# Storing whole output rows for two of four batches, and starting the right half's products between the left half's outputs

## The chip, the cores and the metric

The program runs on one core of one Trainium2 chip, from one launch. A core has a matrix engine (TensorE, PE in the profile, with weight loads shown apart as PEld), a vector engine (DVE), a scalar engine (ACT), GpSimd (POOL), and SyncE (SP), which here issues every transfer. The transfers run on 16 DMA engines between HBM and the on-chip buffer SBUF; matrix products land in a small accumulation memory, PSUM, and have to be copied to SBUF by ACT or DVE before they can be stored. The metric is device microseconds (us) of one execution.

## The reference

Three layers in a row, all in float32, with 4 batches of 448 tokens (1792 rows) and a width of 768:

```python
scores = scale * (q @ k.T) - log(S); x = sigmoid(scores) @ v       # 4 x 12 heads, 448 x 64
x = ((x @ w_a) * (x @ w_b)) @ w_out                                # 1792 x 768, inner 1536
logits = x @ phi                                                   # 1792 x 32 slots
d = softmax of logits over the tokens;  slot_input = d.T @ x       # 32 x 768
for e in range(8):                                                 # 4 slots for each expert
    slot_out[e] = relu(slot_input[e] @ w1[e]) @ w2[e]              # 768 -> 1024 -> 768
c = softmax of logits over the slots
return c @ slot_out                                                # 1792 x 768
```

Only the last two lines are of interest here: the product with w2 gives 32 slot rows of 768 columns, and each of the 1792 tokens gets a weighted sum of those rows. The output is 1792 x 768 x 4 bytes = 5.5 MB.

## The kernel before, in words

One long function, `body`, writes all engines' instructions in program order; a helper (`tc.manual_schedule`) keeps that order on each engine and adds the semaphore waits. Attention, the two large products and the routing statistics take the first 620 us. What follows is bound to the expert weights w1 and w2, which are streamed through a ring of SBUF tiles: `order0`, `order1` and `order2` (L662 to L664) list the transfers, `pump` issues the next one when a ring slot is free, and `done` frees the slots whose tiles have been multiplied.

The end of the program, L813 to L865, is what the change touches:

- `COLS` cuts the 768 output columns into a left half (h = 0) and a right half (h = 1) of 384. The last `NCOL` = 8 entries of `order2`, each 768 KB, are loaded as halves too: L693 issues the eight left halves (384 KB each), then L696 issues the eight right halves. In this document R1 to R8 are those right halves, in order.
- `w2_product(n, halves)` (L816) multiplies four ring tiles, two weight rows of each, into the accumulators `sps[h]` of the halves asked for: eight products for each half, which PE runs as 16 instructions. The last eight tiles take two calls for each half.
- For each half (loop of L844): two calls of `w2_product` finish the sum, then a chain follows with one instruction at a time: a copy out of PSUM (L848, by ACT for the left half and DVE for the right one), a product with `selF` that adds up the four partial sums (L850), a copy again (L851). Then for each chunk `c` of 112 tokens and each batch `b` one small product (L859, two PE instructions) and one copy (L861, ACT for even batches, DVE for odd ones) into an output tile of SBUF. Six PSUM buffers are used in turn (`tags`), so a product waits for the copy of the sixth product before it.
- The left half is stored after every second chunk, for each batch 112 x 2 x 384 numbers (336 KB, L865): 8 transfers, L1 to L8. The right half is stored after each chunk, 112 x 384 numbers (168 KB, L863): 16 transfers. In HBM a stored piece is a run of 384 numbers, 1536 bytes, and the DMA moves it as one packet.

SP issues its transfers in program order, and each waits for the transfer eight places ahead of it to have landed, since eight semaphores are used in turn. On each of the 16 DMA engines transfers are worked off in the order of their issue.

Of the kernel before, what the change touches and what calls it, by code (L numbers as in the profile page):

```python
# [9 lines left out]
F32 = mybir.dt.float32  # L10
# [8 lines left out]
B, H, S, D = 4, 12, 448, 64  # L19
DM, FF, NS, NE, F = 768, 1536, 32, 8, 1024  # L20
C = 4
T = S // C
# [11 lines left out]
def body(ctx, tc, q, k, v, w_a, w_b, w_out, phi, w1, w2, out):  # L34
    nc = tc.nc
    pe, act, dve, pool, sp = nc.tensor, nc.scalar, nc.vector, nc.gpsimd, nc.sync
# [17 lines left out]
    def ps_tile(tag, shape, bufs):  # L54
        return psp.tile(shape, F32, tag=tag, name=tag, bufs=bufs)
# [6 lines left out]
    def ms(shape=(128, S)):  # L62
        tags = banks[run["banks"]]
        tag = tags[run["ms"] % len(tags)]
        run["ms"] += 1
        return ps_tile(tag, list(shape), 4 if tag == "sc" else 2)
# [597 lines left out]
    order2 = [("w2", g, x, j) for g in range(2) for x in range(KE // 2) for j in range(4)]  # L664
    queue = order0 + order1 + order2
    NCOL = 8
    ring, slots, rest = {}, [], []
# [102 lines left out]
    for what in order0:  # L770
        i = what[1]
        h, n, f0 = (0, 4, 4 * i) if i < 3 else (1, 6, 6 * (i - 3))
# [43 lines left out]
    def w2_product(n, halves):  # L816
        _, g, x, _ = order2[n]
        for i in range(2):
            for h in halves:
                c0, w = COLS[h]  # L820
                for j in range(4):
                    pe.matmul(sps[h][32 * j:32 * j + 32], hT[:, 2 * x + i, 2 * j + g],  # L822
                              ring[order2[n + j]][0][:, i, c0:c0 + w],
                              start=(g == 0 and x == 0 and i == 0),
                              stop=(g == 1 and x == KE // 2 - 1 and i == 1))
# [7 lines left out]
    s4, s4r = small[:, :DM], small[:, DM:2 * DM]  # L833
    evac = (act.copy, dve.tensor_copy)
    ov = out.rearrange("(b c p) n -> b p c n", b=B, c=C)
    ob = [[], []]
    for h in range(2):
        for b in range(B):
            pl, nm = slots.pop(0)
            ob[h].append(pl.tile([128, 2048], F32, tag=nm, name="o")[:T, :C * (DM // 2)].rearrange(  # L840
                "p (c n) -> p c n", c=C))
    tags = ("sc", "sc", "sc", "sc", "ms", "ms")
    k = 0
    for h, (c0, w) in enumerate(COLS):  # L844
        for n in range(len(order2) - NCOL, len(order2), 4):
            w2_product(n, (h,))

        evac[h](s4[:, c0:c0 + w], sps[h])  # L848
        t = ms((128, w))
        pe.matmul(t, selF.rearrange("p j s -> p (j s)"), s4[:, c0:c0 + w], start=True, stop=True)  # L850
        evac[h](s4r[:, c0:c0 + w], t)  # L851
        for c in range(C):
            op = []
            for b in range(B):
                tag = tags[k % 6]
                op.append(ps_tile(tag, [T, w], 4 if tag == "sc" else 2))
                k += 1
                r = slice(32 * b, 32 * b + 32)
                pe.matmul(op[b], cT[r, c * T:(c + 1) * T], s4r[r, c0:c0 + w], start=True, stop=True)  # L859
            for b in range(B):  # L860
                evac[b % 2](ob[h][b][:, c], op[b])  # L861
                if h:
                    sp.dma_start(out=ov[b][:, c, c0:c0 + w], in_=ob[h][b][:, c])  # L863
                elif c % 2:
                    sp.dma_start(out=ov[b][:, c - 1:c + 1, c0:c0 + w], in_=ob[h][b][:, c - 1:c + 1])  # L865


# [23 lines left out]
```

## Time and profile before

| | us |
|---|---|
| median of 3 runs (730.11 to 732.01) | 731.52 |
| the profiled execution, its own time | 727.57 |
| span of the profiled execution | 725.5 |
| PE busy | 682.7 (94%) |
| DVE busy, ACT busy | 310.2, 272.0 |
| expert weights and output: DMA engines without a break | from about 633 to the end |

The profiled execution is some 4 us faster than the median of the runs; its own time is 2.07 us over its span. The times in the rows count from the start of the span. The table of engines would call this a PE kernel, but it is an average: PE is the busiest engine for the first 630 us and the DMA engines are for the last 90. The profile's strip of 40 slices (18 us each) shows the change-over, and tables of stretches of 2 us show what holds in the part that the change touches. A DMA share over 1 comes from packets that overlap on one engine.

### The profile page before, as it was taken

The numbers are of one execution on the slowest core, as the hardware profiler recorded it, in microseconds if no ns is written. First come the engines' busy times: TensorE is split into PE (matmuls) and PEld (weight loads), VectorE is DVE, ScalarE is ACT, GpSimd is POOL, SyncE is SP. The second block draws the span as 40 slices with busy tenths as digits, with TensorE's granted clock in tenths as the row PEclk, the third lists the DMA queues.
The fourth block names the chain that finished last, engine by engine and source line by source line (L and its number), as shares of the span: only waits on it lengthen the run. The fifth ranks groups of instructions, "written<-read, shape, count | busy, mean of one in ns | idle before, by whom it ended". The sixth has DMA issues, their size and how long they took to land.

```text
span 725.5 us, 10845 instructions
## 1 busy us (share of the span) xinstructions
PE 682.7 (94%) x4231; PEld 487.8 (67%) x4231; DVE 310.2 (43%) x452; ACT 272.0 (37%) x469; POOL 246.6 (34%) x151
## 2 busy tenths in 40 slices
PE   6999998999999999999999999999999999997684
PEld 4446667777777677688776876877888896433132
DVE  3557998899863323333333232312323232300022
ACT  4778678778643504214135042231201011100021
POOL 0116766666672332233323332323444442100000
PEclk9999999999999999999999999999999999999998
DMA  9967999889962432422414322220689945999998
GB/s 217 196 162 229 301 291 282 280 277 296 298 200 57 128 97 74 128 78 73 133 50 133 106 58 79 88 66 0 243 275 323 366 152 204 394 415 418 412 362 275
DMA packets 107474, 148.99 MB, mean 205 GB/s; under 512 B 51360, under 2 KB 84384, under 8 KB 104352
## 3 DMA queue, kind: packets, MB, share of 16 engines
q1 hardware_dynamic: 107424, 148.31, 63.0%
q8 instruction: 33, 0.54, 0.3%
q14 instruction: 17, 0.14, 0.1%
HBM read 128.46 MB, written 19.83 MB: 204 GB/s over the span
## 4 chain that ended last, share of the span: by engine, by line
PE 77%; DMA 13%; ACT 4%; DVE 3%; issue 1%; POOL 1%; SPq 0%; ACTq 0%; POOLq 0%
PE ab L492 46%; PE sc L193 9%; DMA e<-in_moe_w 9%; PE sc L179 7%; PE ms L147 3%; PE ms L469 2%; ACT a L183 1%; PE ms L455 1%; PE ab L179 1%; PE ms L569 1%; DMA kn<-in_k 1%; DMA out<-w 1%; DVE gk L317 1%; DMA wr_all<-in_moe_w_b 1%; ACT gk L304 1%
## 5 line engine op out<-in xcount | busy, mean ns | idle before, releaser
L420 POOL TENSOR_TENSOR wl<-wr_all,wh 128x768 fp32r<-128x768 f32 x50 | 92.4, 1849 | 204.8 <-DVE wh L419 122.6
L492 PE MATMUL ab<-xh,wh 128*128 128x448 f32 x576 | 142.0, 376 | 1.4 <-ACT wh L419 1.4
L492 PE MATMUL ab<-xh,wl 128*128 128x448 f32 x576 | 141.7, 376 | 0.0
L492 PE MATMUL ab<-xl,wh 128*128 128x448 f32 x576 | 136.2, 371 | 0.0
L492 PEld LDWEIGHTS ab<-xh,wh 128*128 128x128 f32 x576 | 103.2, 188 | 20.9 <-issue 10.9
L492 PEld LDWEIGHTS ab<-xh,wl 128*128 128x128 f32 x576 | 104.0, 188 | 18.3 <-issue 8.6
L492 PEld LDWEIGHTS ab<-xl,wh 128*128 128x128 f32 x576 | 105.9, 188 | 15.5 <-issue 7.3
L183 ACT ACTIVATE a<-sc,nlog 112x448 f32<-112x448 f32 x168 | 93.6, 639 | 59.6 <-PE sc L179 55.9
L322 POOL TENSOR_TENSOR w<-gk,cy 128x768 int32<-128x768 int32 x36 | 66.3, 1841 | 99.5 <-DVE gk L317 72.7
L504 DVE TENSOR_TENSOR misc<-misc,ab 128x448 f32<-128x448 f32 x48 | 29.7, 618 | 127.5 <-PE ab L492 127.4
L501 ACT COPY misc<-ab 128x448 f32<-128x448 f32 x48 | 25.8, 538 | 153.2 <-PE ab L492 148.4
L193 PE MATMUL sc<-a,vn 112*64 112x448 f32 x384 | 76.1, 544 | 0.0
L420 POOL TENSOR_TENSOR wl<-wr,wh 128x768 fp32r<-128x768 f32 x22 | 40.5, 1840 | 53.7 <-DVE wh L419 45.7
L193 PEld LDWEIGHTS sc<-a,vn 112*64 112x64 f32 x384 | 26.0, 137 | 41.5 <-issue 38.7
L419 DVE CAST wh<-wr_all 128x768 fp32r<-128x768 f32 x50 | 35.1, 701 | 37.3 <-POOL wl L420 22.9
L420 POOL TENSOR_TENSOR wl<-w,wh 128x768 fp32r<-128x768 f32 x24 | 45.0, 1873 | 3.0 <-ACT wh L419 3.0
L822 PE MATMUL ab<-e,gk 128*32 128x384 f32 x240 | 34.2, 531 | 11.9 <-DMA e<-in_moe_w 11.7
L204 ACT ACTIVATE xh<-sc 128x448 fp32r<-128x448 f32 x24 | 13.1, 544 | 71.6 <-PE sc L193 71.6
L315 DVE TENSOR_SCALAR mf<-gk 128x768 f32<-128x768 f32 x36 | 34.1, 947 | 9.0 <-ACT gk L304 8.7
L205 DVE TENSOR_TENSOR xl<-sc,xh 128x448 fp32r<-128x448 f32 x24 | 15.0, 623 | 52.3 <-ACT xh L204 52.3
L179 PE MATMUL sc<-qh,kh 64*112 64x448 f32 x168 | 34.9, 411 | 0.6 <-ACT qh L140 0.6
L316 DVE TENSOR_SCALAR gk<-mf 128x768 uint32<-128x768 uint32 x36 | 34.3, 953 | 1.2
(170 smaller groups left out, 745.4 us busy)
## 6 DMA issues: line engine op xcount, KB each, us to landing
e<-in_moe_w SPq DMA_DIRECT2D x23, 1024.0 KB, 7.5
wr_all<-ab SPq DMA_DIRECT2D x50, 384.0 KB, 3.3
e<-in_moe_w SPq DMA_DIRECT2D x23, 768.0 KB, 15.1
wr_cv<-in_moe_w_a SPq DMA_DIRECT2D x12, 768.0 KB, 7.0
wr_all<-in_moe_w_b SPq DMA_DIRECT2D x12, 768.0 KB, 7.0
wr_all<-in_moe_w_out SPq DMA_DIRECT2D x12, 768.0 KB, 6.9
ab<-w SPq DMA_DIRECT2D x24, 384.0 KB, 7.0
wr<-ab SPq DMA_DIRECT2D x22, 384.0 KB, 3.7
```

Of the source, the lines that this page charges most:

```text
L179: pe.matmul(sc[h], kx[r, cs], qx[r], start=(i == 0), stop=(i == 2))
L183: act.activation(a, sc[h], AF.Sigmoid, bias=nlog[:T], scale=1.0 / math.sqrt(D))
L193: pe.matmul(pv_t[g][64 * h:64 * h + 64], qkv_t["v", g][:, h, c, :], a_t.pop((g, h, c)), start=(c == 0), stop=(c == C - 1))
L315: dve.tensor_scalar(mf, m, LOW, HIGH, op0=ALU.max, op1=ALU.min)
L316: dve.tensor_scalar(mi, mf.bitcast(U32), 3, 0x3FFFFFFF, op0=ALU.logical_shift_left, op1=ALU.bitwise_and)
L322: pool.tensor_tensor(thirds(w), m.bitcast(I32), thirds(cy_t.pop(x)), op=ALU.add)
L419: rnd(wh, t)
L420: pool.tensor_tensor(wl, t, wh.bitcast(F32), op=ALU.subtract)
L492: pe.matmul(t, w[:, kk * 128:(kk + 1) * 128], xt[b * NP + kk][xi], start=(s == 0 and kk == 0), stop=(s == 2 and kk == KD - 1))
L501: act.copy(gT_all[n % 5], t)
L504: dve.tensor_tensor(g, g, t, op=ALU.mult)
L822: pe.matmul(sps[h][32 * j:32 * j + 32], hT[:, 2 * x + i, 2 * j + g], ring[order2[n + j]][0][:, i, c0:c0 + w], start=(g == 0 and x == 0 and ...
```

## The change

Four things move, and no arithmetic changes.

1. Batches 2 and 3 (`b >= NH`) get output tiles of whole rows, for two chunks each: the left copy writes columns 0 to 383 of the tile and the right copy columns 384 to 767. Nothing of them is stored in the left half's turn. In the right half's turn, after each chunk, one transfer stores 112 whole rows of 768 numbers (336 KB, runs of 3072 bytes).
2. Batches 0 and 1 are stored as before: left half for two chunks at a time, right half for each chunk.
3. The first `w2_product` of the right half (tiles R1 to R4) stands between the left outputs of chunk 1 and those of chunk 2. Only the second one (R5 to R8) is left ahead of the right half's chain.
4. The tiles come from the same free slots in another order (`o_tile`).

Stores are 4 of 336 KB (runs of 1536 bytes), 8 of 168 KB (1536) and 8 of 336 KB (3072): 20 instead of 24.

```diff
-    ob = [[], []]
-    for h in range(2):
-        for b in range(B):
-            pl, nm = slots.pop(0)
-            ob[h].append(pl.tile([128, 2048], F32, tag=nm, name="o")[:T, :C * (DM // 2)].rearrange(
-                "p (c n) -> p c n", c=C))
+    NH = 2
+    def o_tile(c):
+        pl, nm = slots.pop(0)
+        return pl.tile([128, 2048], F32, tag=nm, name="o")[:T, :1536].rearrange("p (c n) -> p c n", c=c)
+    ob = {(h, b): o_tile(C) for h in range(2) for b in range(NH)}
+    ob.update({(c, b): o_tile(2) for b in range(NH, B) for c in range(0, C, 2)})
...
         for n in range(len(order2) - NCOL, len(order2), 4):
-            w2_product(n, (h,))
+            if h == 0 or n + 4 == len(order2):
+                w2_product(n, (h,))
...
+            if h == 0 and c == 1:
+                w2_product(len(order2) - NCOL, (1,))
             for b in range(B):
-                evac[b % 2](ob[h][b][:, c], op[b])
-                if h:
-                    sp.dma_start(out=ov[b][:, c, c0:c0 + w], in_=ob[h][b][:, c])
+                o = ob[h, b][:, c] if b < NH else ob[c // 2 * 2, b][:, c % 2, c0:c0 + w]
+                evac[b % 2](o, op[b])
+                if b >= NH:
+                    if h:
+                        sp.dma_start(out=ov[b][:, c], in_=ob[c // 2 * 2, b][:, c % 2])
+                elif h:
+                    sp.dma_start(out=ov[b][:, c, c0:c0 + w], in_=o)
                 elif c % 2:
-                    sp.dma_start(out=ov[b][:, c - 1:c + 1, c0:c0 + w], in_=ob[h][b][:, c - 1:c + 1])
+                    sp.dma_start(out=ov[b][:, c - 1:c + 1, c0:c0 + w], in_=ob[h, b][:, c - 1:c + 1])
```

On PE, between the left half's chain and the right half's, the order before was this (sc and ms are the PSUM buffers of the outputs, gk_95 holds the slot rows, misc the combine weights; the rows of L822 are the right products, here with the tiles of R1 to R4):

```order
L850 MATMUL ms<-gk_95,selF 128x384
L859 MATMUL sc<-gk_95,misc 112x384 x4
L859 MATMUL ms<-gk_95,misc 112x384 x2
L859 MATMUL sc<-gk_95,misc 112x384 x4
L859 MATMUL ms<-gk_95,misc 112x384 x2
L859 MATMUL sc<-gk_95,misc 112x384 x4
L822 MATMUL ab<-e_6129,gk_95 32x384
L822 MATMUL ab<-e_6131,gk_95 32x384
L822 MATMUL ab<-e_6149,gk_95 32x384
L822 MATMUL ab<-e_6151,gk_95 32x384
```

All 16 outputs came first, then the right products. At the same place PE now has:

```order
L863 MATMUL sc<-gk_95,misc 112x384 x2
L822 MATMUL ab<-e_6129,gk_95 32x384
L822 MATMUL ab<-e_6131,gk_95 32x384
L822 MATMUL ab<-e_6149,gk_95 32x384
L822 MATMUL ab<-e_6151,gk_95 32x384
L822 MATMUL ab<-e_6129,gk_95 32x384
L822 MATMUL ab<-e_6131,gk_95 32x384
L822 MATMUL ab<-e_6149,gk_95 32x384
L822 MATMUL ab<-e_6151,gk_95 32x384
L863 MATMUL sc<-gk_95,misc 112x384 x2
L863 MATMUL ms<-gk_95,misc 112x384 x2
L863 MATMUL sc<-gk_95,misc 112x384 x4
```

The eight products with R1 to R4 moved ahead of the last eight left outputs (chunks 2 and 3); those with R5 to R8 stay behind them. On SP, at the end of its queue, the stores follow the last right weight tile; before and after in one piece:

```order
 L696 DMA e_6175<-in_moe_w 128x2x384
-L865 DMA out<-o 112x2x384 x8
-L863 DMA out<-o 112x384 x16
-L887 UNCONDITIONAL_BRANCH
+L875 DMA out<-o 112x2x384 x4
+L873 DMA out<-o 112x384 x2
+L871 DMA out<-o 112x768 x2
+L873 DMA out<-o 112x384 x2
+L871 DMA out<-o 112x768 x2
+L873 DMA out<-o 112x384 x2
+L871 DMA out<-o 112x768 x2
```

Four of the eight left stores are gone, and every chunk of the right turn stores two half rows and two whole rows (a fourth such pair follows the piece).

## Rows read from the trace of the kernel before

**Rows 1.** The profile's strip of 40 slices, DMA engines' busy share in tenths.

```profile
DMA  9967999889962432422414322220689945999998
```

**Rows 2.** Stretches of 2 us: engines' busy time, granted clock, DMA share, GB/s.

```profile
702.00:704.00 2.00, 1.78 (x14) 0.96 (x16) 0.81 (x2) 1.02 (x4) 0.00 (x0) 1.00 1.07 375
...
708.00:710.00 2.00, 1.43 (x20) 0.34 (x12) 0.51 (x1) 0.00 (x0) 0.00 (x0) 1.00 1.03 336
...
712.00:714.00 2.00, 2.00 (x20) 1.18 (x16) 1.30 (x3) 1.24 (x3) 0.00 (x0) 1.00 0.97 316
...
720.00:722.00 2.00, 0.00 (x0) 0.00 (x0) 0.00 (x0) 0.00 (x0) 0.00 (x0) 0.50 0.87 280
...
724.00:725.50 1.50, 0.00 (x0) 0.00 (x0) 0.00 (x0) 0.00 (x0) 0.00 (x0) 0.50 0.01 2
```

**Rows 3.** Chain of waits, order of time: start, length, what.

```profile
690.22 8.37 DMA e<-in_moe_w
...
698.63 1.49 PE ab L822 x10
...
706.71 2.76 PE ab L822 x32
...
709.49 0.57 DVE gk L848
...
711.73 0.58 PE ms L859 x2
```

**Rows 4.** DMA issues at 694.4 (R4), 698.6, 710.4, 713.2, 721.9: us to landing.

```profile
e<-in_moe_w SPq DMA_DIRECT2D x1, 384.0 KB, 9.2
...
e<-in_moe_w SPq DMA_DIRECT2D x1, 384.0 KB, 9.1
...
out<-o SPq DMA_DIRECT2D x1, 336.0 KB, 4.6
...
out<-o SPq DMA_DIRECT2D x1, 168.0 KB, 2.2
...
out<-o SPq DMA_DIRECT2D x1, 168.0 KB, 2.6
```

**Rows 5.** SP's issues: R8 (timeline), then L865, L863 (durations, first and last start).

```profile
698.61 0.37 SPq L696 DMA_DIRECT2D e<-in_moe_w  x1
...
L865 SPq DMA_DIRECT2D out<-o x8: 351/638/1195, 704.4 to 710.3; - x8
...
L863 SPq DMA_DIRECT2D out<-o x16: 331/393/923, 713.2 to 721.9; - x16
```

**Rows 6.** Timeline of the left outputs on PE, then ACT: start, length, instructions.

```profile
702.22 0.91 PE L859 MATMUL sc<-gk,misc 32*112 32x384 f32 x8 [0.57 <-ACT gk L851]
...
703.68 1.16 PE L859 MATMUL sc<-gk,misc 32*112 32x384 f32 x6
...
703.15 0.86 ACT L861 COPY o<-sc 112x384 f32<-112x384 f32 x2 [0.98 <-PE sc L859]
...
706.07 0.86 ACT L861 COPY o<-sc 112x384 f32<-112x384 f32 x2 [0.22 <-PE sc L859]
```

**Rows 7.** DMA view, 204.8 to 207.2: one store, rows of 3072 bytes, nothing else.

```profile
DMA packets 144, 0.39 MB, mean 164 GB/s; under 512 B 16, under 2 KB 16, under 8 KB 144
...
q1 hardware_dynamic: 144, 0.39, 41.6%
...
ab<-w SPq DMA_DIRECT2D x1, 384.0 KB, 2.3
```

**Rows 8.** DMA view, 708 to 712 (left stores), then 716 to 724 (right stores).

```profile
DMA packets 916, 1.31 MB, mean 328 GB/s; under 512 B 61, under 2 KB 916, under 8 KB 916
...
q1 hardware_dynamic: 916, 1.31, 100.8%
...
DMA packets 1660, 2.23 MB, mean 278 GB/s; under 512 B 211, under 2 KB 1660, under 8 KB 1660
...
q1 hardware_dynamic: 1660, 2.23, 86.5%
```

## The prediction

> **What bounds the kernel now.** I read the strip of slices first: from the 35th slice on the DMA engines are full to the end [rows 1], so in the last 90 us PE's 94% says nothing. Then the stretches of 2 us: DMA share 1.07 while the last weights come (375 GB/s), 1.03 and 0.97 while left outputs are stored (336, 316), 0.87 in the right outputs' turn (280), and nothing after 724 [rows 2]. The chain of waits shows how the two turns hang together: the last left weight tile lands at 698.59 (690.22 + 8.37), PE needs 1.49 us after it, then come copies and outputs; the right half's products stand at 706.71 for 2.76 us and end at 709.47, and its chain has its first output product at 711.73 [rows 3]. Single issues give the ends: R4 is issued at 694.4 and lands 9.2 later, at 703.6; R8 at 698.61 + 9.1 = 707.7; the last left store at 710.35 + 4.6 = 714.95; the last right store at 721.88 + 2.6 = 724.48 [rows 4, 5]. The program's end waits for that last landing, 1.0 us ahead of the span's end. So the question is one sum: when does the last store land?
>
> From 707.7 to 724.48 the DMA engines have 24 stores, with no break between the turns, because the first right store (713.16) comes before the last left one has landed. In the left turn eight stores take 714.95 - 707.7 = 7.25 us, 0.91 each; in the right turn 16 take 724.48 - 714.95 = 9.53, 0.595 each. Twice 0.595 is 1.19, so for the same bytes the small stores are dearer.
>
> **The change, part by part.**
>
> *Price of a packet.* From 708 to 712, 855 packets of 1536 bytes (916 less 61 tiny ones) take 1.008 x 16 x 4 us = 64.5 us of engine time, 75 ns each; from 716 to 724 it is 0.865 x 16 x 8 / 1449 = 76 ns [rows 8]. Packets of 3072 bytes stored alone: 0.416 x 16 x 2.4 / 128 = 125 ns [rows 7]. A whole row is 125 ns against 2 x 75. A store of 112 rows gives each engine 7 packets, so 7 x 25 = 0.175 us less than 14 packets of half rows.
>
> The Trainium skill, "DMA: Bandwidth & Descriptors", Specifications, gives 512 bytes as the smallest transfer for line rate, which both lengths pass; the rows do not agree, 20.5 bytes per ns at 1536 and 24.6 at 3072, and what the rule would mean here is rival 2.
>
> *Price of a whole-row store.* The trace has none in a full queue, so I bound it. From the left turn: 0.91 - 0.175 = 0.735. From the right turn: 0.595 + 7 x 0.050 = 0.945. Below 0.735 no row reaches. I take the middle, 0.84: it has the seven packets of the right turn and the bytes of the left turn. A half-row store of 168 KB keeps its 0.595; bound below, half of the left turn's, 0.455.
>
> *The product moved forward.* Four PE instructions of the six at 703.68 are chunk 1's, so PE comes to it at about 704.4 [rows 6], after R4 (703.6): no wait. It takes half of 2.76 us [rows 3], to 705.75. Chunks 2 and 3 come behind: the first copy starts 0.93 us after the first product (703.15 against 702.22), so at 706.7, where in the old order ACT was at its last two copies (706.07) [rows 6]. With 0.43 to 0.48 each on ACT, batch 0's second left store is issued at about 708.1, batch 1's (DVE) at 708.4. PE's last left product waits for the second copies (707.2) and is through at about 707.6. Batches 2 and 3 have no left store to delay.
>
> *The right half's chain.* Its last eight products need R8, 707.7. By the left half's row PE then needs 1.49 us more [rows 3]: 709.2. By PE alone it is 707.6 + 1.4 + the last one's length, 709.3. Before it was 709.47. So the move gains 0.2 us, not the 1.4 us that it takes off the end: R8's landing is next late, and the left copies, which it pushed back. The first right store goes out at 713.16 - 0.2 = 712.95.
>
> *The break.* Only four left stores are left. Numbers 3 and 4 (issued at 708.1 and 708.4) run alone: by the lone store, 2.3 us for 8 packets of 125 ns, so 1.3 us besides the packets [rows 7]; 14 packets of 75 ns make 2.35 us, which is 710.5 and, one store later, 711.4. Then nothing is queued until 712.95. A right store alone lands after 1.3 + 7 x 0.075 = 1.85 us (2.2 in the row behind the left stores [rows 4]), at 714.8. Some 3 us of DMA time that the old order filled stand empty.
>
> *SP.* It has 4 issues fewer. Issues of 112 rows had a median of 393 ns [rows 5], four for each chunk 1.6 us, against 2 x 0.595 + 2 x 0.84 = 2.9 us of DMA: no limit. Each waits for the one eight places ahead, 5.7 us of DMA work: none either. Copies make a chunk in 1.0 us (three of them from 703.15 to 706.07 on ACT [rows 6]). The tiles' new order costs nothing: they come from slots whose weights were multiplied before the last eight tiles, as before, and what ACT's copies wait for is PE [rows 6]; uncovered, it would be one copy, 0.5 us.
>
> *Sum.* First right store lands at 714.8; seven more half-row stores at 0.595 (4.2) and eight whole-row stores at 0.84 (6.7) give 725.7, against 724.48: **1.2 us later**. On the profiled execution 727.57 becomes 728.8; on the median, 731.52 + 1.2 = 732.7. Lower bounds (0.455 and 0.735): 714.8 + 3.2 + 5.9 = 723.9, or 0.6 faster; upper (0.595 and 0.945): 726.5, or 2.0 slower.
>
> **The rivals.**
>
> 1. *The stores flow as densely as in the left turn.* For it: share 1.03 there against 0.87 later, and a right turn in which every engine starts level and the queue is fed faster than it empties. Against it: the 0.87 was reached with a queue (landing 2.2 to 2.6 us after the issue where 1.85 would be alone), so it looks like a cost of each transfer, of which the new right turn has as many, 16. It gives the lower bound, 0.6 us faster: 730.9.
>
> 2. *Whole rows save nothing, so the break counts in full: slower.* Place: the eight whole-row stores behind one another. Price: 2 x 0.595 = 1.19 each instead of 0.84, 2.8 us over the eight, so 728.5 for the last landing, 4.0 us later: 735.5. It decides from 0.595 x 2 down to about 0.97 for one store; above that the kernel is more than 0.3% slower. For it: no store of whole rows of this output stands in the trace, and bytes could be what counts in a full queue. Against it: 125 ns against 150 [rows 7, 8]. The rule above, under which both lengths run at line rate, comes to this rival.
>
> 3. *The break does not come.* If the left stores drain more slowly than I say, or the right chain is earlier, the engines stay at work between the turns: four stores at 0.91, eight at 0.595 and eight at 0.84 behind 707.7 end at 722.8, 1.7 us earlier than before: 729.8. Against it: at 0.91 the four are done by 711.4 even on the last engine, and R8's landing at 707.7 holds the right chain where it is.
>
> **How the numbers follow.** A measurement of this kernel can tell about 0.3% (2.2 us) from no change. Forecast (1.2 slower, between its bounds) 0.68; rival 1 0.13; rival 2 0.13; rival 3 0.06. The likeliest gives 732.7. Slower by over 0.3% holds rival 2 and the forecast's upper edge with the runs' own spread (they lie from 1.4 below to 0.5 above their median): 0.17. Faster by over 0.3% needs rivals 1 or 3 with a drift of the runs on top: 0.05. Within it: 0.78. The range runs from 730.3 (rival 1 with 0.6 of spread; most of rival 3 is left out) to 734.6 (upper bound 733.5 and 1.1 of spread, which leaves most of rival 2 out).
>
> **What would show it.** Right: a hole in the DMA share between about 711 and 713.5; first right store near 713; whole-row stores landing 0.75 to 0.95 us apart; the last landing 1 us later than before. PE's second right product starting at R8's landing shows why the moved product gains nothing. Wrong: no hole (rival 3), whole-row packets near 150 ns or landings 1.1 apart (rival 2), a DMA share of 1.0 in the right turn (rival 1), or right products that end well before 709.

## The result, and the profile after

The changed kernel is slower: 736.24 us median (732.33 to 738.36, 10 runs) against 729.84 us (728.34 to 732.01, 10 runs) of the kernel before. The ratio of the runs is 1.0079 (95% interval 1.0059 to 1.0098), which is 5.8 us (4.3 to 7.2); the two medians are 6.4 apart. The forecast was 1.2 us slower, within what can be told from no change; the time lies above the range's end of 734.6 and next to rival 2's 735.5.

The profiled execution of the changed kernel took 735.85 us, with a span of 733.8. Part of that is not the change's: the code up to the last weight tiles is the same in all kernels here, and yet in 12 traces the last left weight tile landed anywhere from 698.6 to 709.8 us. So this text compares **tails**: the time from the landing of the last left weight tile to the landing of the last store. Before it is 724.48 - 698.59 = 25.9 us [rows 3, 4]. After, the chain of waits gives the tile's landing, 693.76 + 8.37 = 702.13, and how the tail goes on:

```profile
693.76 8.37 DMA e<-in_moe_w
...
708.24 1.43 PE ab L822 x16
...
710.51 1.57 PE sc L863 x8
712.08 1.47 PE ab L822 x16
...
714.27 0.90 PE ms L854 x2
```

The first right product now stands at 708.24, between the left outputs, and only the second one (712.08) is left ahead of the right half's chain. SP's issues in the timeline (start, time from the first issue's start to the last one's end, how many) and, below, the times from issue to landing of R8 (issued at 702.15), of the last left store (712.5) and of the first and the last right store:

```profile
707.95 4.88 SPq L875 DMA_DIRECT2D out<-o  x4
717.24 0.80 SPq L873 DMA_DIRECT2D out<-o  x2
...
728.04 0.92 SPq L871 DMA_DIRECT2D out<-o  x2
...
e<-in_moe_w SPq DMA_DIRECT2D x1, 384.0 KB, 8.2
...
out<-o SPq DMA_DIRECT2D x1, 336.0 KB, 3.4
...
out<-o SPq DMA_DIRECT2D x1, 168.0 KB, 2.1
...
out<-o SPq DMA_DIRECT2D x1, 336.0 KB, 4.3
```

The first right store goes out at 717.24, 15.1 us into the tail (14.6 before), and lands at 719.4. The last one is issued at 728.55 and lands 4.3 later, at 732.8: a tail of **30.7 us, 4.8 more**. Stretches of 2 us, to be read beside [rows 2] (the last two columns are the DMA share and GB/s):

```profile
710.00:712.00 2.00, 2.00 (x16) 0.75 (x8) 1.43 (x3) 1.25 (x4) 0.00 (x0) 1.00 0.53 185
712.00:714.00 2.00, 1.50 (x17) 0.42 (x16) 1.04 (x3) 0.47 (x1) 0.00 (x0) 1.00 0.66 190
714.00:716.00 2.00, 1.08 (x6) 0.49 (x10) 0.68 (x2) 0.00 (x0) 0.00 (x0) 1.00 0.47 159
716.00:718.00 2.00, 2.00 (x18) 1.18 (x16) 1.22 (x3) 1.24 (x3) 0.00 (x0) 1.00 0.00 0
718.00:720.00 2.00, 2.00 (x18) 1.48 (x14) 1.88 (x5) 1.58 (x4) 0.00 (x0) 1.00 0.90 273
...
726.00:728.00 2.00, 0.00 (x0) 0.00 (x0) 0.00 (x0) 0.00 (x0) 0.00 (x0) 0.50 0.95 308
```

The break is there, a whole stretch without one packet (716 to 718) and half-filled ones before it. Behind it the stores run at 273 to 317 GB/s in the stretches up to 730, little faster than the half rows before, which ran at 279 to 301 from 714 to 722.

### The profile page after: what moved, and what is told of

Read it like the earlier page. It is cut to its first block, busy times and chain, and to the rows that moved or that the text cites. A ratio compares the mean times of both kernels' runs of the same rounds, so it can differ in the third digit from the quotient of the medians.

```text
span 733.8 us, 10838 instructions
## 1 busy us (share of the span) xinstructions
PE 686.2 (94%) x4231; PEld 488.3 (67%) x4231; DVE 305.0 (42%) x452; ACT 272.2 (37%) x469; POOL 248.5 (34%) x151
## 4 chain that ended last, share of the span: by engine, by line
PE 77%; DMA 14%; ACT 3%; DVE 3%; issue 1%; SPq 0%; ACTq 0%
PE ab L492 45%; PE sc L193 10%; DMA e<-in_moe_w 9%; PE sc L179 7%; PE ms L147 3%; PE ms L469 2%; DMA wr_all<-in_moe_w_b 2%; DMA kn<-in_k 1%; PE ms L455 1%; ACT a L183 1%; PE ms L569 1%; PE ab L179 1%; DMA wr_cv<-in_moe_w_a 1%; DVE gk L317 1%; PE sc L863 1%
## 5 line engine op out<-in xcount | busy, mean ns | idle before, releaser
L322 POOL TENSOR_TENSOR w<-gk,cy 128x768 int32<-128x768 int32 x36 | 66.1, 1836 | 99.4 <-DVE gk L317 69.5
L501 ACT COPY misc<-ab 128x448 f32<-128x448 f32 x48 | 25.7, 535 | 153.1 <-PE ab L492 148.3
L420 POOL TENSOR_TENSOR wl<-w,wh 128x768 fp32r<-128x768 f32 x24 | 47.1, 1964 | 3.1 <-ACT wh L419 3.1
L822 PE MATMUL ab<-e,gk 128*32 128x384 f32 x240 | 35.8, 562 | 12.1 <-DMA e<-in_moe_w 12.1
## 6 DMA issues: line engine op xcount, KB each, us to landing
e<-in_moe_w SPq DMA_DIRECT2D x23, 768.0 KB, 15.1
```

What stands on the lines that cost most here:

```text
L322: pool.tensor_tensor(thirds(w), m.bitcast(I32), thirds(cy_t.pop(x)), op=ALU.add)
L420: pool.tensor_tensor(wl, t, wh.bitcast(F32), op=ALU.subtract)
L501: act.copy(gT_all[n % 5], t)
```

## The experiments

Tails and times in one table first. "First" is the landing of the first right store, counted in the tail; the ratio is of the times to the kernel before.

| kernel | first | tail | ratio (95% interval) |
|---|---|---|---|
| before | 16.8 | 25.9 | |
| changed kernel | 17.2 | 30.7 | 1.0079 (1.0059 to 1.0098) |
| e1_move | 17.3 | 25.7 | 1.0021 (1.0000 to 1.0043) |
| e2_rows | 16.7 | 30.0 | 1.0056 (1.0035 to 1.0076) |
| e3_split | 17.2 | 30.7 | 1.0082 (1.0051 to 1.0113) |
| e4_pairs | 18.5 | 25.8 | 0.9997 (0.9978 to 1.0016) |
| e5_rows128 | 16.3 | 24.4 | 0.9989 (0.9960 to 1.0018) |
| e6_one_batch | 17.2 | 28.6 | 1.0026 (0.9998 to 1.0053) |
| e8_flat128 | 16.2 | 23.2 | 0.9948 (0.9932 to 0.9963) |
| e10_flat128_rows | 16.2 | 26.4 | 1.0011 (0.9994 to 1.0029) |

Each tail is read from one execution. In two further traces with the unchanged tail (the probes below) it is 26.1 and 25.7, so it repeats to about 0.2 us either way. The times repeat less well, since what lies ahead of the tail varies. The ratios are of the runs as a whole; a quotient of two medians can differ from them by a tenth of a per cent.

**The two halves of the change apart.** e1_move moves the product alone:

```diff
-            w2_product(n, (h,))
+            if h == 0 or n + 4 == len(order2):
+                w2_product(n, (h,))
...
+            if h == 0 and c == 1:
+                w2_product(len(order2) - NCOL, (1,))
```

> Only the moved product: the right half's first eight products (R1 to R4) stand between the left outputs of chunks 1 and 2, all 24 stores are those of the kernel before. Call tail the time from the landing of the last left weight tile to the landing of the last store: 25.9 us before, 30.7 us after the whole change. Theory A (the loss comes from bytes that wait behind a break in the stores, and from whole rows that save nothing): the right chain starts 0.5 us later, as in the changed kernel, but four left stores more fill the time until then; tail 25.9 to 27, ratio to the kernel before 1.000 to 1.002. Theory B (the moved product is what costs, since it holds back the left copies and through them the right chain): tail 29 to 31, ratio 1.004 or more.

The right chain came later, as in the changed kernel (first right store issued 15.1 us into the tail), but the tail did not grow: 25.7. SP's issues show why, eight left stores up to 716.8 and the right ones from 718.87, so the DMA engines have work until the right half's chain is through. Their share is 0.99 and 1.01 in the two stretches shown below the issues; at that place of its tail (712 to 716) the changed kernel had 0.66 and 0.47:

```profile
709.58 7.19 SPq L868 DMA_DIRECT2D out<-o  x8
718.87 8.25 SPq L866 DMA_DIRECT2D out<-o  x16
...
714.00:716.00 2.00, 1.23 (x17) 0.37 (x10) 0.85 (x2) 0.09 (x1) 0.00 (x0) 1.00 0.99 320
716.00:718.00 2.00, 1.35 (x10) 0.60 (x12) 0.56 (x1) 0.00 (x0) 0.00 (x0) 1.00 1.01 328
```

The time was 1.0021 of before, an interval that begins at no change; its trace shows nothing of that in the tail.

e2_rows is the other half, the changed kernel with both right products where they were (the two edits above undone).

> Only the stores of the change: whole rows for batches 2 and 3, the right products where they were before. Theory A: nearly the whole loss, less the 0.5 us by which the right chain came later; tail 29.5 to 30.5, ratio 1.005 to 1.008. Theory B: tail 26 to 27, ratio at most 1.002.

The tail is 30.0 and the ratio 1.0056, so the loss is in the stores. Without the moved product its first right store lands 0.5 us earlier, and its break is as empty:

```profile
712.00:714.00 2.00, 1.23 (x10) 0.30 (x2) 0.56 (x1) 0.00 (x0) 0.00 (x0) 1.00 0.54 182
714.00:716.00 2.00, 1.35 (x13) 0.64 (x12) 0.67 (x2) 0.15 (x1) 0.00 (x0) 1.00 0.00 0
```

So theory A held: by these tails the stores cost 4.1 us, and the moved product 0.5 to 0.7 more, only where the stores don't cover it.

**Do whole rows save anything?** e3_split keeps the order of the changed kernel and writes each whole row as two halves:

```diff
-                        sp.dma_start(out=ov[b][:, c], in_=ob[c // 2 * 2, b][:, c % 2])
+                        for x0, xw in COLS:
+                            sp.dma_start(out=ov[b][:, c, x0:x0 + xw], in_=ob[c // 2 * 2, b][:, c % 2, x0:x0 + xw])
```

> The changed kernel with each whole-row store written as two stores, one of the left 384 columns and one of the right: the same bytes at the same place, in runs of 1536 instead of 3072 bytes, 28 stores instead of 20. If a whole-row store saves nothing for its bytes (its landings were 1.19 us apart, twice the 0.595 of a half-row store): tail 30.2 to 31.2, as in the changed kernel. If it saves what I forecast (0.84 against 1.19): tail 33 to 34, ratio to the kernel before 1.011 or more. It also bears on SP: 24 issues of 0.4 us in the right turn are 9.6 us, less than the 13.5 us of the stores.

The tail is the same to a tenth, 30.7. The DMA views of the two right turns, first the changed kernel from 720 to 732, then e3_split from 721 to 733:

```profile
DMA packets 1716, 3.57 MB, mean 297 GB/s; under 512 B 219, under 2 KB 891, under 8 KB 1716
...
q1 hardware_dynamic: 1716, 3.57, 90.7%
...
DMA packets 2605, 3.50 MB, mean 292 GB/s; under 512 B 328, under 2 KB 2605, under 8 KB 2605
...
q1 hardware_dynamic: 2605, 3.50, 90.1%
```

The first has 825 packets of 3072 bytes and 672 of 1536, the second 2277 of 1536, and both move 292 to 297 GB/s at the same share. Taking 75 ns for a packet of 1536 bytes, and, as a guess, 2 us for the 219 small packets (with nothing for them the result is 150), the 0.907 x 16 x 12 = 174 us of the first leave (174 - 672 x 0.075 - 2) / 825 = 148 ns for one of 3072: twice the other, and not the 125 that I had read from the lone store. SP is cleared as well: 28 issues or 20 made no difference.

**Does the number of bytes moved count, or the break as such?** e6_one_batch sets `NH = 3`, so that whole rows and their wait are one batch's.

> The changed kernel with whole rows for one batch only (NH = 3). Accounting by theory A: each 168 KB that is moved out of the left turn adds 0.595 us at the end, since the left turn's stores lie in a stretch that the right half's chain takes anyway; four of them instead of eight, so tail 25.8 + 2.4 = 28.2, ratio 1.004 to 1.006. If the break had a price of its own, independent of its bytes (a queue that runs dry and starts again): tail 29.5 or more.

The tail is 28.6. From e1_move, which has the same chain, that is 2.9 us for four times 168 KB that left the left turn, and 5.0 for eight: 0.62 to 0.73 each, near the 0.595 of a right store. The loss goes in the main with the bytes. A line through the two tails with a break meets no bytes at all at 26.5, 0.8 us above e1_move's 25.7; that is little more than such tails scatter, and a price of that size for the break itself is not excluded.

**Why were the small stores dearer?** In the kernel before 336 KB had cost, as I read it, 0.91 in the left turn and 1.19 in the right one. e4_pairs stores the right half in pairs too (the condition `if h` and its store are left out, so that `c % 2` decides for both halves).

> The kernel before with the right half stored in pairs of chunks as the left half is: 8 stores of 336 KB instead of 16 of 168 KB, all runs of 1536 bytes. If a store has a cost of its own (0.595 for 168 KB against 0.91 for 336 KB, so 0.27 for each store): eight stores fewer save about 2 us, less 1 us since the first right store waits for a second chunk; tail 24.5 to 25.5, ratio 0.998 to 0.9995. If a steady rate for stores bounds the turn (294 GB/s in the changed kernel, 284 before): nothing is saved and the first store comes later; tail 26 to 27, ratio 1.000 to 1.002.

Neither expectation held as a whole. The first store landed 1.7 us later, at 18.5, and the tail was still 25.8: seven more stores took 7.3 us, 1.04 each, against 1.19 for two single ones. Larger stores save 0.15 us each, and the wait for the second chunk gives it back. That is no way out either. It also shows that the 0.91 was too low: from 707.7 to 714.95 the DMA engines of the kernel before moved 2.31 MB in all, and the eight left stores are 2.75 MB, so part of them had been moved before R8's last packets landed. By the 328 GB/s of [rows 8] a left store of 336 KB took 1.05 us, as the large stores of e4_pairs did.

**The store's price by itself.** e7_probe adds groups of stores behind the kernel's end, to a scratch tensor, each group behind a wait for the one before.

> The kernel before with groups of stores added behind its end, to a scratch tensor, each group behind a wait for the one before: one store of 112 whole rows (768 numbers); 8 of them; 16 of 112 half rows (384); 8 of two chunks of 112 half rows; one of 128 whole rows; 8 of them; 16 of 128 half rows; one of 128 whole rows. Only the rates of the groups are read. Theory P: the groups of 112 rows run at 280 to 330 GB/s even alone, those of 128 rows at 370 to 400, and whole rows differ little from half rows. Theory Q: lone stores of either kind have packets of 120 to 125 ns, groups of either kind 145 to 155 ns and about 300 GB/s. If whole rows do save time in a queue of nothing but whole rows, the group of 8 x 112 whole rows is 15% faster than that of 16 half rows.

The stretches lie inside five groups (112 whole rows, 112 half rows, two chunks of 112 half rows, 128 whole rows, 128 half rows); DMA share and GB/s are the last columns:

```profile
735.00:742.00 7.00, 0.00 (x0) 0.00 (x0) 0.00 (x0) 0.00 (x0) 0.00 (x0) 0.50 0.96 315
748.00:754.00 6.00, 0.00 (x0) 0.00 (x0) 0.00 (x0) 0.00 (x0) 0.00 (x0) 0.50 0.96 307
761.00:767.00 6.00, 0.00 (x0) 0.00 (x0) 0.00 (x0) 0.00 (x0) 0.00 (x0) 0.50 1.00 316
776.00:782.00 6.00, 0.00 (x0) 0.00 (x0) 0.00 (x0) 0.00 (x0) 0.00 (x0) 0.50 1.02 397
788.00:794.00 6.00, 0.00 (x0) 0.00 (x0) 0.00 (x0) 0.00 (x0) 0.00 (x0) 0.50 1.04 367
```

This decides it for theory P: under theory Q the groups of 128 rows would have run at about 300 too. With 112 rows the length of a run hardly matters (315, 307, 316 GB/s); with 128 rows everything is faster, half rows 367, whole rows 397. The DMA view of the two groups of whole rows gives the packet: 0.961 x 16 x 7 / 717 = 150 ns with 112 rows, 1.023 x 16 x 6 / 775 = 127 ns with 128:

```profile
DMA packets 819, 2.20 MB, mean 315 GB/s; under 512 B 102, under 2 KB 102, under 8 KB 819
...
q1 hardware_dynamic: 819, 2.20, 96.1%
...
DMA packets 871, 2.38 MB, mean 397 GB/s; under 512 B 96, under 2 KB 96, under 8 KB 871
...
q1 hardware_dynamic: 871, 2.38, 102.3%
```

The store that I had priced the change with [rows 7] has 128 rows. The stores of the change have 112. A store of 112 rows that runs alone was not measured: the first one of the probe was issued at 726.81, when the kernel's own last store (landing at 729.7) was still under way.

e9_probe_rows asks which numbers of rows are cheap.

> The kernel before with groups of eight stores of whole rows added behind its end, each group behind a wait: 112, 96, 64, 32, 128 and 120 rows. Only the groups' rates are read. If 128 is the favoured number because each DMA engine then has four or eight rows that lie in one port of the buffer: 112, 96 and 120 rows have packets of 140 to 155 ns, 128 rows 126 ns, and 64 and 32 rows, which reach half of the ports, twice the 126 or so. If a fraction of the engines or the bytes alone mattered: 96 and 112 rows lie between 64 and 128 in proportion to their rows.

Inside the groups of 96, 64, 32, 128 and 120 whole rows:

```profile
737.00:745.00 8.00, 0.00 (x0) 0.00 (x0) 0.00 (x0) 0.00 (x0) 0.00 (x0) 0.50 0.95 290
750.00:756.00 6.00, 0.00 (x0) 0.00 (x0) 0.00 (x0) 0.00 (x0) 0.00 (x0) 0.50 1.00 201
760.00:764.00 4.00, 0.00 (x0) 0.00 (x0) 0.00 (x0) 0.00 (x0) 0.00 (x0) 0.50 0.84 190
768.00:774.00 6.00, 0.00 (x0) 0.00 (x0) 0.00 (x0) 0.00 (x0) 0.00 (x0) 0.50 1.02 396
780.00:788.00 8.00, 0.00 (x0) 0.00 (x0) 0.00 (x0) 0.00 (x0) 0.00 (x0) 0.50 0.88 308
```

Half the rows, 64, run at 201, half of 396. In proportion to the rows between these two, 96, 112 and 120 would reach 298, 347 and 372: 96 rows come near it with 290, while 112 (315 in e7_probe) and 120 (308) stay well below. The packets, worked out as above, take 245 ns with 64 rows, 161 with 96, 150 with 112, 140 with 120 and 127 with 128. The 120 are a case apart: their eight stores have 120 small packets, 15 for each, where those of 96 rows have 128, and the DMA share is 0.88, so it looks as if one of the 16 engines had none of their work. The expectation named 140 to 155 ns for the three numbers in between, and twice 126 for 64 and 32; 96 rows and 32 (218 ns) miss that.

The Trainium skill, "SBUF — State Buffer", Door 1: The DMA port swizzle, says that 64 partitions reach only 8 of the buffer's 16 ports, and gives about 218 GB/s as what 64 or 32 can get; 201 and 190 here are in line with it. Its table has no range between 64 and 128. By the same skill, "DMA: Bandwidth & Descriptors", Rules for kernel authors, an outermost dimension that is a multiple of 16, ideally the 128 partitions, uses all 16 engines, and 112 is such a multiple; the share of 0.96 agrees, and the rate of 315 against 397 shows that all 16 engines at work are not enough for the rate of 128 rows. Why 112 and 120 rows are slower than their number says was not tried apart and stays open.

**Stores of 128 rows in the kernel.** e5_rows128 cuts each batch into chunks of 128, 128, 128 and 64 tokens instead of four of 112.

```diff
+        for c in range(3):
...
+                pe.matmul(op[b], cT[r, c * 128:(c + 1) * 128], s4r[r, c0:c0 + w], start=True, stop=True)
...
+        for b in range(0, B, 2):
+            op = next_ps(w)
+            for i in range(2):
...
+                pe.matmul(op[64 * i:64 * i + 64], cT[r, 384:S], s4r[r, c0:c0 + w], start=True, stop=True)
```

> The kernel before with its output cut in other chunks of tokens: 128, 128, 128 and 64 of each batch instead of four of 112; the 64s of two batches share one accumulation tile. Stores are 384 KB or 192 KB of 128 rows and 96 KB of 64 rows, all in runs of 1536 bytes, 8 rows of a chunk for each DMA engine instead of 7. Theory P (112 rows are laid over the buffer's partitions so that DMA engines stand in each other's way, which is why stores in a queue run at 284 to 294 GB/s and the lone one of 128 rows at about 390): packets stay near 62 to 66 ns, the right turn takes 7.5 to 8.5 us instead of 9.5, tail 24 to 25, ratio 0.997 to 0.999. Theory Q (a queue of stores has a steady rate, whatever the rows): tail 25.5 to 26.5, ratio 0.9995 to 1.002.

The tail is 24.4, 1.5 less, as theory P has it; the time, 0.9989, can't be told from before. Its 64-row stores are the weak part: the last four, 96 KB each, landed 0.4 to 0.7 us apart, where 192 KB in 128 rows took 0.54.

e8_flat128 has none of them: the 1792 rows are cut into 14 chunks of 128 whatever the batch, and two chunks are put together from 64 rows of one batch and 64 of the next.

```diff
+        for cs in ((0, 4, 7, 11), (1, 5, 8, 12), (2, 6, 9, 13), (3, 10)):
...
+                while at < end:
+                    b, t0 = divmod(at, S)
+                    n = min(end - at, S - t0)
+                    r = slice(32 * b, 32 * b + 32)
+                    p0 = at - 128 * c
+                    pe.matmul(op[-1][p0:p0 + n], cT[r, t0:t0 + n], s4r[r, c0:c0 + w], start=True, stop=True)
+                    at += n
```

> The kernel before with its 1792 output rows cut into 14 chunks of 128 rows, without regard to batches (two of them take 64 rows of one batch and 64 of the next, by two products into one accumulation tile). Left half: six stores of two chunks and two of one; right half: 14 stores of 192 KB; all runs of 1536 bytes. If stores of 128 rows keep in the kernel the price that they had in the groups by themselves (0.535 us for 192 KB, against 0.576 for 168 KB of 112 rows): first right store lands 16.2 us after the last left weight tile, 13 more at 0.535 make a tail of 23.2 against 25.9 before, ratio 0.995 to 0.998. If the kernel's stores are bound by something else in the tail: 25 to 26, ratio 0.999 to 1.001.

The tail is 23.2, as worked out, and the time 726.38 us against 729.80, with a ratio of 0.9948: 0.5% and clear of no change, **faster than both kernels**. Of the 2.7 us that the tail lost, 0.6 lie ahead of the first right landing and 2.1 behind it. It also has two right stores fewer than the kernel before, which at e4_pairs' 0.15 us for each would be 0.3. Its right turn, 14 stores from 713.69, and two stretches of it:

```profile
713.69 6.78 SPq L873 DMA_DIRECT2D out<-o  x14
...
716.00:718.00 2.00, 0.48 (x8) 0.00 (x0) 0.83 (x2) 0.48 (x1) 0.00 (x0) 0.98 1.04 365
718.00:720.00 2.00, 0.00 (x0) 0.00 (x0) 0.00 (x0) 0.00 (x0) 0.00 (x0) 0.50 1.04 368
```

368 GB/s where the kernel before has 280 [rows 2].

e10_flat128_rows puts the change's storing into this kernel: whole rows, with the wait, for the last seven chunks.

> The kernel with 14 chunks of 128 rows, and the change's storing in it: the last seven chunks in whole rows (384 KB, runs of 3072 bytes) in the right turn, none of their left half in the left turn; no product is moved. By the groups a whole-row store of 128 rows takes 0.989 us against 2 x 0.535. If the loss of the change is the work moved behind the break, it shows here too although whole rows now save 8%: first right store at 16.2, then 6 x 0.535 + 7 x 0.989, tail about 26.5, 3 us more than the same kernel without it, ratio 0.999 to 1.002. If whole rows make up for the break once the rows are 128: tail 23 to 24, ratio as that kernel's.

The tail is 26.4, 3.2 more than without and what the groups' prices gave. Whole rows do save something here (378 to 396 GB/s in the stretches of the right turn from 718 on, half and whole rows mixed, against 365 to 369), and it does not pay for the break, which is in the trace again:

```profile
712.00:714.00 2.00, 1.23 (x14) 0.33 (x6) 0.56 (x1) 0.00 (x0) 0.00 (x0) 1.00 0.41 151
714.00:716.00 2.00, 1.35 (x12) 0.69 (x12) 0.56 (x1) 0.03 (x1) 0.00 (x0) 1.00 0.00 0
...
718.00:720.00 2.00, 1.27 (x12) 0.21 (x8) 1.62 (x4) 1.17 (x3) 0.00 (x0) 1.00 1.03 394
```

## Why the prediction was wrong, point by point

*What bounds the kernel:* right. All that the change did to the stores is in the last 31 us and hangs on when the last store lands; SP played no part (e3_split has eight more issues and the same tail), and no run shows an effect of the tiles' order.

*The price of a whole-row store: this step failed.* The prediction took 125 ns for a packet of 3072 bytes from the one lone store of the trace and built both ends of its range on it, 0.735 and 0.945, with 0.84 between. In the changed kernel seven half-row and eight whole-row stores behind the first one took 732.8 - 719.4 = 13.4 us; with 0.595 for a half-row store a whole-row store took 1.15, and the packet 148 ns. What made the lone store cheap was not that it was alone, since a group of eight such stores has packets of 127 ns, and not its long runs by themselves, which at 112 rows are worth next to nothing (150 ns against 2 x 76). It was that it had 128 rows: there two half rows take 2 x 69.5 = 139 ns and a whole one 127. The prices of half rows are from the same groups of e7_probe, 0.955 x 16 x 6 / 1198 and 1.038 x 16 x 6 / 1434. The upper end should have been twice 0.595, the price that the same bytes had in that very stretch; I had put it aside as a rival. Of the 3.6 us between the forecast's tail and the measured one, 8 x (1.15 - 0.84) = 2.5 are this term. The lower end was too low for a second reason, the 0.91 of a left store, which was about 1.05.

*The product moved forward: mis-sized, and with the wrong sign.* Forecast was a gain of 0.2 us for the right chain; it came 0.5 later. Two estimates behind it were off. R8 is not what is late next: it landed 8.2 us into the tail (702.15 + 8.2 = 710.4), not 9.1 as in the trace of before; it did so, to 0.1 us, in ten of the 12 traces, with the old stores too, and the one that I had read was the odd one. And the left outputs of chunks 2 and 3 took until 712.0, 9.9 into the tail, where I had 9.0: behind the moved product the copies start late (ACT at 710.53, 8.4 into the tail, where I had 8.1) and PE ends its last product 1.55 us after that, where I had 0.9. That is 0.7 us of the 3.6; another 0.3 is that the first right store took 2.1 us to land and not 1.85.

*The break:* right in place and cause, too small in size. The left stores were done at 715.9, the first right packet came after 718, and the DMA engines were empty between. I had counted some 3 us of DMA time left empty; by the shares from 710 to 718 (0.53, 0.66, 0.47 and 0.00) it was 4.7 in that stretch. What the prediction did not say plainly is the account that e6_one_batch and e2_rows bear out: since the right turn can't begin earlier, each 168 KB taken out of the left turn comes back as about one right store, 0.5 to 0.7 us, and eight right stores at 0.595 are 4.8 us. Whole rows would have had to win all of that back, and at the forecast's 0.84 they would have won 2.8.

*Rival 2* (whole rows save nothing) is what happened: its last landing is 4.0 us later, against 4.8 measured. That its 735.5 comes so near 736.24 is partly luck, since it starts from a median of 731.52 where ten runs gave 729.84. The step that gave it 0.13 was the comparison "125 ns against 150", a store of 128 rows against stores of 112. *Rival 1:* the share in the right turn stayed at 0.9. *Rival 3:* the break came.

## What to carry to other kernels

A price read from one row of a trace holds for the shape in that row: check partitions as well as bytes and run length before using it for a new store, and let a range reach to what the same bytes cost in the stretch itself. Where a tail is bound by stores and a chain in it can't start earlier, stores that are put off past the chain come back nearly in full (4.1 to 5.0 us here for 4.8 us of right stores); make them cheaper where they stand. Here that was the number of rows: chunks of 128 instead of 112, with the left turn and the right turn as they were, gave 0.5%.

## What the runs showed of the hardware

That stores from 96 or 112 partitions run at 290 to 316 GB/s and those from 128 at 367 to 397, with the DMA engines' share at 0.95 or more in all of them, was not expected; nor that 120 partitions gain nothing over 112 (308 GB/s at a share of 0.88); nor that a run of 3072 bytes is worth 8% over one of 1536 at 128 rows and next to nothing at 112. A store of twice the size saved 0.15 us in the queue (e4_pairs), not the 0.27 that I had read from the two turns of the kernel before.
